# Spectral block on one core: where the second weights' second half is converted, and where the first inverse run stands

## The chip, the cores and the metric

The kernel runs on one core of one Trainium2 chip. The metric is the time of one execution on the device in microseconds (us). Before the change the median of three runs is 1846.89 us (1846.84 to 1847.31). TensorE (PE) multiplies matrices; VectorE (DVE), ScalarE (ACT) and GpSimd (POOL) work on tiles; all DMAs are issued from the queue of SyncE (SP).

## The reference

For x of shape (8, 3136, 256): a real FFT along the sequence, a complex 256x256 channel mix with bias, a soft threshold of 0.01, and the inverse FFT. On its result the second block: u = x + real(FFT2(x)), a layer norm, a two-layer MLP (256 to 1024 to 256) with relu, and the residual. Cut to what matters:

```
X = rfft(x, axis=1)
Y = soft(Xr @ w_r - Xi @ w_i + b_r) + 1j * soft(Xr @ w_i + Xi @ w_r + b_i)
x = irfft(Y, n=3136, axis=1)
u = x + real(fft(fft(x, axis=1), axis=2))
out = u + relu(norm(u) @ w_ch1) @ w_ch2
```

## The kernel before, in words

**Sequences and stages.** The eight sequences (b = 0 to 7) go through ten tasks each, which the code calls p1, p2_f2, p2_w, p2_mix, p2_yt, p2_g2, p3_norm, p3_tr, p3_mlp1 and p3_mlp2. The FFT of 3136 is split into 64 x 49. `p1` is the 64-point step and stores ad (for b = 0: aq) to DRAM. `p2_*` run over q = 0 to 3, four stages of eight frequency slots: `p2_f2` (L503) loads af and the table tff and does the 49-point step (L527), `p2_w` (L559) the channel products g_w, bias and soft threshold (ks L585, y L590, m L592, Y L593), `p2_mix` the channel FFT for the mixed part (ef or eo L631, mq) and its stores md, `p2_yt` (L704) transposes Y (L730), and `p2_g2` the inverse 49-point step, evicted as bev (L761) and stored as bd (L763). `p3_norm` (L774) loads bf from bd and mt from md, does the inverse 64-point step with `quarters` (L405, matmuls L410), adds mt (L779, tile ut) and takes the norm's statistics. `p3_tr` (L847) transposes ut to uth and utl (L861 to L863), `p3_mlp1` (L865) makes h, hh and hl, `p3_mlp2` (L890) makes o and the output. Sequence 0 works in plain fp32; from b = 1 on an operand is a pair of fp32r tiles (h and l) and a product is three matmuls (`mm3`, L170).

**Order.** Each task is a generator that yields due times in units of T. A heap takes the task with the lowest due time, and what it traces up to its next yield comes next; `after(keys)` (L313) puts a task off by 10 of these units until the keys have been marked in `done`. The constants at the top (SHAPE, STEP, T1, WTIMES, NRM, TR and others) set the due times. The framework then fixes the order of each engine, and of SP's queue, in a simulated timeline in which earlier traced work has priority and tiles of one tag get their rooms in turn; on the chip each engine takes its instructions in that order. `tc.issue_after(x)` puts an instruction behind x on the same engine. `behind(key, ...)` (L305) issues a load on SP behind the DMA that `af_ld[key]` names; af_ld[0] to af_ld[7] are the af loads of sequence 0, two for each q.

**The weights.** `weights` (L917) loads the MLP's weights, which come as 64-bit numbers, in eight raw pieces (k = 0 to 7; 0 to 3 for w1, 4 to 7 for w2), and `split_double` (L182) turns a piece into h and l: one activation on ACT (L200), seven operations on DVE (L201, L203, L205, L207, L209, L220, L221) and one cast on ACT (L219). The temporaries are two tiles in the mt rooms (there are two) and two in the ut rooms (there are four). The four pieces of w2 are called its parts 1 to 4 here. Their raw tiles have the two uth rooms; their ACT activation stands behind the last ks of sequence 0's stage q = 2 (parts 1 and 2) or q = 3 (parts 3 and 4). w2's results have the rooms W2 and W3, which `p1` of b = 1 uses for its xf before.

**The first inverse.** For b = 0 the first run of `quarters` is traced after the mark ("w", 1, 0), and its first matmul is put on PE behind the last W product of the second sequence's stage q = 0 (L837, L841). The others are put behind that one.

```
if b == 0 and ms[0] == 0:
    yield from after(("w", 1, 0))
...
quarters(inv_f, groups, w_in[1, 0] if b == 0 and ms[0] == 0 else None)
```

Of the kernel before, what the change touches and what calls it, by code (L numbers as in the profile page):

```python
# [20 lines left out]
D = 256  # L21
# [117 lines left out]
SHAPE, STEP1, STEP = (0.395, 0.569, 0.36), 0.2, 0.25  # L139
START1, LEAD, LAST = 1.61, 1.53, 0.05  # L140
T1, ASK, BEHIND = (1.25, 0.17), 1.16, 3
WTIMES = (1.002, 1.003, 1.151, 1.152, 1.4, 1.44, 1.54, 1.57)
MLAG, NRM, TR = 1.874, -1.239, -0.86


# [1 line left out]
def spectral_block(ctx: ExitStack, tc: tile.TileContext, x, w_ri, b_ri, w1, w2,  # L147
# [169 lines left out]
    def n2_rows(t, m, n):  # L317

        return t[m:m + n].rearrange("n r c u d -> (r c u) n d")
# [183 lines left out]
    def p2_f2(b):  # L503


        for q in range(4):
            base, STEP, F2W, W0, WW, M0 = clock2(b, q)
            u0 = 8 * q
            yield base
            yield from after(("a", b, q) if b == 0 else ("a", b))  # L510
            if b == 0:
                X = sb.tile([128, 2, 2, 8, S], F32, tag=("Xh", "Xl")[q % 2], bufs=1, name="X")
                Xs = sb.tile([128, 2, 8, S], F32, tag=("Xsh", "Xsl")[q % 2], bufs=1, name="Xs")
                xt[b, q] = X, Xs
            else:
                xt[b, q] = Xh, Xl, Xsh, Xsl = x_tiles()
            afs, tfs = zip(*[rows_f2(b, q, s) for s in range(2)])
            for ui in range(4):
                yield base + STEP * ui * F2W / 4
                us = slice(ui * 2, ui * 2 + 2)  # L520
                lo_x = lo_v if b == 1 and q == 0 else lo_g
                g = gtile("g_f2")
                gf = g[:, :400].rearrange("p (k c s j) -> p k c s j", k=2, c=2, s=2)
                for s in range(2):
                    yield base + STEP * F2W * (ui / 4 + s / 8)
                    for k in range(2):
                        mm = te.matmul(gf[:, k, :, s], afs[s][:, ui * D + k * 128:ui * D + k * 128 + 128],  # L527
                                  tfs[s][:, ui].rearrange("p (c j) -> p c j", c=2), start=True, stop=True)
                    if b == 0 and q == 0 and ui == 0:
                        f2_in[s] = mm.ins  # L530
                        done.add(("f2", s))
                gv = g[:, :400].rearrange("p (k c t) -> p k c t", k=2, c=2)

                def view(t):
                    return t[..., us, :].rearrange("p k c s j -> p k c (s j)" if len(t.shape) == 5 else "p k s j -> p k (s j)")

                if b == 0:
                    xv_ = view(X)
                    sc.copy(xv_, gv)
                    va.tensor_add(view(Xs), xv_[:, :, 0], xv_[:, :, 1])  # L540
                    continue
                xs = sb.tile([128, 2, 2 * S], F32, tag="xs", bufs=2, name="xs")
                xh, xl, xsh, xsl = (view(t) for t in (Xh, Xl, Xsh, Xsl))
                if ui < 3:
                    xx = sb.tile([128, 2, 2, 2 * S], F32, tag="xx", bufs=2, name="xx")
                    sc.copy(xx, gv)
                    sc.copy(xh, xx)  # L547
                    lo_x(xl, xx, xh)
                    va.tensor_add(xs, xx[:, :, 0], xx[:, :, 1])
                else:  # L550
                    im = sb.tile([128, 2, 2 * S], F32, tag="im", bufs=1, name="im")
                    sc.copy(xh, gv)
                    sc.copy(im, gv[:, :, 1])
                    va.tensor_add(xs, gv[:, :, 0], im)
                    lo_v(xl, gv, xh)
                sc.copy(xsh, xs)
                lo_x(xsl, xs, xsh)
# [146 lines left out]
    def p2_yt(b):  # L704

        for q in range(4):
            base, STEP, F2W, W0, WW, M0 = clock2(b, q)
            u0 = 8 * q
            yield base + STEP * M0
            y = yt_[b, q]  # L710
            for i in range(4):
                yield base + STEP * (M0 + 0.022 + 0.185 * i)
                s = i // 2
                if i % 2 == 0:
                    tif = sb.tile([100, 4, 98], F32, tag="tif", bufs=2, name="tif")
                    behind(3 if b or q else 1, out=tif, in_=c_ti[:, u0 + 4 * s:u0 + 4 * s + 4, :])
                    if b == 0:
                        tabs[b, q, s] = tif, None
                    else:
                        tih = sb.tile([100, 4, 98], F32R, tag="tih", bufs=1, name="tih")  # L720
                        til = sb.tile([100, 4, 98], F32R, tag="til", bufs=1, name="til")
                        with tc.issue_after(ks_in[b, q]):
                            sc.copy(tih, tif)
                        lo_v(til, tif, tih)
                        tabs[b, q, s] = tih, til
                gt = gtile("g_yt")
                for v in range(2):
                    place = 2 * (2 * (i % 2) + v) + s
                    for o in range(2):
                        te.transpose(gt[:100, (v * 2 + o) * 128:(v * 2 + o + 1) * 128],  # L730
                                     y[:, o, place].rearrange("p c j -> p (c j)"), ident)
                if b == 0:
                    yf = sb.tile([100, 512], F32, tag=("yh", "yl")[i % 2], bufs=2, name="yf")
                    sc.copy(yf, gt[:100])
                    yhl[b, q, i] = yf, None
                    continue
                yh = sb.tile([100, 512], F32R, tag="yh", bufs=2, name="yh")
                yl = sb.tile([100, 512], F32R, tag="yl", bufs=2, name="yl")
                sc.copy(yh, gt[:100])
                lo_v(yl, gt[:100], yh)  # L740
                yhl[b, q, i] = yh, yl
# [32 lines left out]
    def p3_norm(b):  # L774
# [31 lines left out]
        def load(m, n):  # L806
            mt = sb.tile([128, 4, D], F32, tag="mt", bufs=2, name="mt")
            bfs = [sb.tile([128, 512], F32, tag="bf", bufs=4, name="bf") for _ in range(1 + (n > 1))]
            for r in range(2):
                if n == 1:  # L810
                    nc.sync.dma_start(out=bfs[0][64 * r:64 * r + 64, :D], in_=b_dram[b - 1 + r][m, 0].rearrange("c u d -> (c u) d"))
                else:
                    nc.sync.dma_start(out=bfs[r].rearrange("p (n d) -> p n d", d=D), in_=n2_rows(b_dram[b], m + 2 * r, 2))
            for r in (1, 0):
                bb, n2 = (b - 1 + r, m) if n == 1 else (b, NM * r + m)
                mpn, mmn = (d[0:NH].rearrange("(a n2) d -> a n2 d", n2=N2) for d in m_dram[bb])
# [6 lines left out]
        for ms in pairs + [[NM - 1]] * (b % 2):  # L823
            n = 1 if ms[0] == NM - 1 else 4
            t0, T3 = clock3(b, ms[0])
            yield t0 + T3 * (NRM - 0.5 * (n == 1))
            yield from after(("b", b), ("m", b))
            loads = [load(m, n) for m in ms]
            if n == 1:
                mt, bfs = loads[0]  # L830
                g = gtile("g_g1")
                te.matmul(g[:, :D], inv_f, bfs[0][:, :D], start=True, stop=True)
                add(ms[0], 1, g, mt[:, :1])
                finish(ms[0], 1)
                continue
            if b == 0 and ms[0] == 0:
                yield from after(("w", 1, 0))  # L837
            groups = [([gtile("g_g1") for _ in range(2)], [[bfs[r][64 * p:64 * p + 64] for r in range(2)] for p in range(2)], bfs[0][0:1, 0:2])
                      for mt, bfs in loads]
            quarters(inv_f, groups, w_in[1, 0] if b == 0 and ms[0] == 0 else None)  # L840
            parts = [(m + 2 * p, g, mt[:, 2 * p:2 * p + 2]) for m, (mt, bfs), (banks, movs, late) in zip(ms, loads, groups) for p, g in enumerate(banks)]  # L841
            for m, g, mt in parts:
                add(m, 2, g, mt)
            for m, g, mt in parts:
                finish(m, 2)

    def p3_tr(b):  # L847
        for gi, (g0, z) in enumerate(GROUPS[b % 2]):
            t0, T3 = clock3(b, g0)
            w = z * 128  # L850
            for k in range(2):
                yield t0 + T3 * (TR + k / 4)
                if k == 0:
                    uth = sb.tile([128, 2, 512], F32R, tag="uth", bufs=UTHB, name="uth")
                    utl = sb.tile([128, 2, 512], F32R, tag="utl", bufs=2, name="utl")
# [61 lines left out]
    def weights():  # L917
# [8 lines left out]

        def load(k):
            i, name, sl, src = todo[k]
            tag = "utl" if k in (2, 3) else "uth"
            raw = raws[k] = sb.tile([128, 1024], I32, tag=tag, bufs=2 if tag == "utl" else UTHB, name="raw_" + name)  # L930
            behind(("q1", "q1", 3, 3, 5, 5, 5, 5)[k], out=raw.rearrange("p (f e) -> p f e", f=src.shape[1]), in_=src)
        for k, (i, name, sl, src) in enumerate(todo):
            yield T * WTIMES[k]
            yield from after("q1")
# [4 lines left out]
                l = sb.tile(shape, F32R, tag=f"W{2 * i + 1}", bufs=1, name=name + "l")  # L939
                mlp_w[name] = h, l  # L940
            if i:
                split_double(name, h, l, [(sl, raws.pop(k))], False, ks_in[0, 2 + (k > 5)])
            elif k % 2:
                mark = (0, k // 2)
                yield from after(("w",) + mark)
# [69 lines left out]
```

## Time and profile before

| | |
|---|---|
| median of three runs | 1846.89 us |
| the profiled execution's own time | 1843.13 us |
| its span, first to last instruction | 1841.2 us |
| mean granted TensorE clock | 0.993 |
| PE busy | 1798.6 us, 98% |
| DVE busy | 1200.5 us, 65% |
| ACT busy | 807.7 us, 44% |
| POOL busy | 561.8 us, 31% |

Times in the rows are microseconds from the span's start. In a timeline, each line has the start, the duration, the engine, the line of the kernel, the operation, the tiles and a count; what stands in brackets is the idle time of the engine before it and what ended that. Neighbouring instructions of an engine overlap a little. The profiled execution is one run; its own time stands 3.76 us below the median of the others.

### The profile page before, as it was taken

The page shows a single profiled execution, that of the slowest core. Times are in us where ns is not written, and L with a number is a line of the kernel's source. Part 1 is how long each engine was busy: PE and PEld are TensorE (multiplying, and loading weights), DVE is VectorE, ACT ScalarE, POOL GpSimd, SP SyncE. Part 2 cuts the span into 40 slices and gives each one's busy share as a digit, 9 for nine tenths or more (in the row PEclk, how much of TensorE's full clock was granted, in tenths as well). Part 3 has the DMA queues.
Part 4 walks back from the last instruction along what each step waited for, and adds up shares of the span by engine and source line. Part 5 has one row for each costly group of instructions (what it writes and reads, how often), then busy time and mean ns, then how long its engine had stood idle before and what let it go on. Part 6 is the DMA issues. An engine that isn't in the chain of part 4 may idle for free.

```text
span 1841.2 us, 29453 instructions
## 1 busy us (share of the span) xinstructions
PE 1798.6 (98%) x10087; PEld 1498.7 (81%) x10087; DVE 1200.5 (65%) x2619; ACT 807.7 (44%) x1911; POOL 561.8 (31%) x1021
## 2 busy tenths in 40 slices
PE   8987999999999999999999999999999999999998
PEld 5566778888888988888888888888888898878888
DVE  3685686676577766765776667757657767655543
ACT  2664545444445534444444444444444454432222
POOL 0002434333234333343432343423324344222110
PEclk9998999999999999999999999999999999999999
DMA  8856564444436543374515744346533533152211
GB/s 247 272 173 165 165 178 135 148 137 138 130 82 198 159 123 104 97 212 125 172 47 135 215 132 125 104 129 164 159 99 86 169 94 112 56 150 69 59 35 33
DMA packets 157934, 245.61 MB, mean 133 GB/s; under 512 B 24208, under 2 KB 105176, under 8 KB 157528
## 3 DMA queue, kind: packets, MB, share of 16 engines
q1 hardware_dynamic: 157784, 243.72, 45.3%
q8 instruction: 80, 1.31, 0.3%
q14 instruction: 70, 0.57, 0.1%
HBM read 140.79 MB, written 102.86 MB: 132 GB/s over the span
## 4 chain that ended last, share of the span: by engine, by line
PE 86%; DVE 5%; DMA 4%; ACT 1%; SPq 1%; issue 1%; POOL 1%; DVEq 0%; ACTq 0%; POOLq 0%
PE o L175 28%; PE h L175 27%; PE g_w L175 9%; PE g_f L527 5%; PE g_g L175 4%; PE g_yt L730 3%; PE g_g L410 2%; PE g_ut L861 2%; PE g_f L410 2%; PE g_mix L667 1%; DMA out_dram<-total 1%; PE g_f L372 1%; DMA aq<-ev 1%; PE g_mix L669 1%; PE g_w L576 1%
## 5 line engine op out<-in xcount | busy, mean ns | idle before, releaser
L880 DVE SCALAR_TENSOR_TENSOR hl<-h,hh 128x512 fp32r<-128x512 f32 (+2 forms) x416 | 272.1, 655 | 391.2 <-ACT hh L879 386.8
L879 ACT ACTIVATE hh<-h 128x512 fp32r<-128x512 f32 (+2 forms) x416 | 237.7, 572 | 505.7 <-PE h L175 459.4
L175 PE MATMUL o<-hl,w2h 128*128 128x512 f32 (+2 forms) x832 | 328.9, 395 | 2.0 <-DVE hl L880 1.5
L175 PE MATMUL h<-utl,w1h 128*128 128x512 f32 (+2 forms) x832 | 319.0, 383 | 1.3 <-DVE utl L165 1.3
L175 PE MATMUL o<-hh,w2l 128*128 128x512 f32 (+2 forms) x832 | 317.9, 382 | 0.0
L175 PE MATMUL o<-hh,w2h 128*128 128x512 f32 (+2 forms) x832 | 317.3, 381 | 0.0
L175 PE MATMUL h<-uth,w1l 128*128 128x512 f32 (+2 forms) x832 | 316.0, 380 | 0.0
L175 PE MATMUL h<-uth,w1h 128*128 128x512 f32 (+2 forms) x832 | 315.3, 379 | 0.0
L887 POOL TENSOR_TENSOR total<-uth,utl 128x256 f32<-128x256 f32 x200 | 149.6, 772 | 460.6 <-DMA out_dram<-total 244.9
L175 PEld LDWEIGHTS o<-hl,w2h 128*128 128x128 f32 x832 | 156.7, 188 | 49.3 <-DVE hl L880 18.7
L175 PEld LDWEIGHTS h<-utl,w1h 128*128 128x128 f32 x832 | 156.8, 188 | 30.5 <-DVE utl L165 1.7
L175 PEld LDWEIGHTS h<-uth,w1l 128*128 128x128 f32 x832 | 156.7, 188 | 29.5 <-issue 1.6
L175 PEld LDWEIGHTS h<-uth,w1h 128*128 128x128 f32 x832 | 156.9, 189 | 27.7 <-issue 2.4
L175 PEld LDWEIGHTS o<-hh,w2l 128*128 128x128 f32 x832 | 156.5, 188 | 27.2
L175 PEld LDWEIGHTS o<-hh,w2h 128*128 128x128 f32 x832 | 156.9, 189 | 19.8 <-issue 0.8
L527 PE MATMUL g_f<-tff,af 98*128 98x100 f32 x1024 | 139.9, 276 | 2.1 <-DMA af<-aq 1.3
L527 PEld LDWEIGHTS g_f<-tff,af 98*128 98x128 f32 x1024 | 134.2, 195 | 7.8 <-issue 1.7
L593 POOL TENSOR_TENSOR Y<-y,m 128x400 f32<-128x400 f32 x56 | 66.9, 1194 | 208.4 <-DVE m L592 198.6
L590 DVE SCALAR_TENSOR_TENSOR y<-g_w,small,ks 128x400 f32<-128x400 f32 x128 | 80.4, 629 | 54.3 <-PE g_w L175 38.0
L168 POOL TENSOR_TENSOR Xl<-xx,Xh 128x400 fp32r<-128x400 f32 x81 | 88.4, 1092 | 60.3 <-ACT Xh L547 56.8
L761 ACT COPY bev<-g_g 98x512 f32<-98x512 f32 x128 | 74.7, 585 | 40.2 <-PE g_g L175 29.3
L730 PE MATMUL g_yt<-ident,Y 128*100 128x128 f32 x512 | 81.8, 277 | 4.8 <-DVE Y L593 4.6
(162 smaller groups left out, 3269.7 us busy)
## 6 DMA issues: line engine op xcount, KB each, us to landing
bd<-bev SPq DMA_DIRECT2D x128, 196.0 KB
mt<-md SPq DMA_DIRECT2D x192, 128.0 KB
bf<-bd SPq DMA_DIRECT2D x96, 256.0 KB
out_dram<-total SPq DMA_DIRECT2D x88, 256.0 KB
af<-ad SPq DMA_DIRECT2D x56, 392.0 KB
ad<-xf SPq DMA_DIRECT2D x84, 256.0 KB
md<-mq SPq DMA_DIRECT2D x112, 192.0 KB
xf<-in_x SPq DMA_DIRECT2D x39, 512.0 KB
```

The source lines that it names most:

```text
L168: gp.tensor_sub(out_, full, hi.bitcast(F32))
L175: last = te.matmul(o, l, r, start=start and i == 0, stop=stop and i == 2)
L410: return te.matmul(banks[i][64 * j:64 * j + 64], mat[rows, rows], movs[i][j], start=True, stop=True)
L527: mm = te.matmul(gf[:, k, :, s], afs[s][:, ui * D + k * 128:ui * D + k * 128 + 128], tfs[s][:, ui].rearrange("p (c j) -> p c j", c=2), sta ...
L590: va.scalar_tensor_tensor(y1, gw, bias[:, c, o:o + 1], ks, op0=ALU.add, op1=ALU.add)
L593: (va if b == 0 or o == 0 else gp).tensor_sub(y[:, o, :, c, :], y1, m)
L730: te.transpose(gt[:100, (v * 2 + o) * 128:(v * 2 + o + 1) * 128], y[:, o, place].rearrange("p c j -> p (c j)"), ident)
L761: sc.copy(bev, g[:98])
L861: te.transpose(gv[:, i], ut[:, j, k * 128:(k + 1) * 128], ident)
L879: sc.activation(hh[:, :w], h[:, :w], AF.Relu)
L880: va.scalar_tensor_tensor(hl[:, :w], h[:, :w], 0.0, hh[:, :w].bitcast(F32), op0=ALU.max, op1=ALU.subtract)
L887: gp.tensor_add(total[:, k, cols], uth[:, k, cols].bitcast(F32), utl[:, k, cols].bitcast(F32))
```

## The change

Parts 1 and 2 of w2 are placed behind ks of stage q = 1 and q = 2 of sequence 0 (before: q = 2 for both); parts 3 and 4 behind the last ks of stage q = 0 of the second sequence (before: q = 3 of sequence 0). The raw tiles of parts 3 and 4 get the two tot rooms, and their loads follow af_ld[7] in place of af_ld[5]. The task waits for the W stage's mark before it traces a conversion. The first inverse run is traced, and put on PE, behind the last f2 matmul of the second sequence's stage q = 1. The tif loads of the second sequence's stage q = 0 are traced after the first load of `p3_norm` and issued behind its bf load; the first transposes of u are traced after the first group of `p3_norm`. Four due times of w2's parts change.

```diff
-WTIMES = (1.002, 1.003, 1.151, 1.152, 1.4, 1.44, 1.54, 1.57)
+WTIMES = (1.002, 1.003, 1.151, 1.152, 1.36, 1.42, 1.6, 1.61)
...
@@ p2_f2
                         f2_in[s] = mm.ins
                         done.add(("f2", s))
+                    if b == 1 and q == 1 and ui == 3 and s == 1:
+                        f2_in["last"] = mm.ins
+                        done.add("f2")
...
@@ p2_yt
                 if i % 2 == 0:
+                    if b == 1 and q == 0:
+                        yield from after("norm")
                     tif = sb.tile([100, 4, 98], F32, tag="tif", bufs=2, name="tif")
-                    behind(3 if b or q else 1, out=tif, in_=c_ti[:, u0 + 4 * s:u0 + 4 * s + 4, :])
+                    behind("bf" if b == 1 and q == 0 else 3 if b or q else 1, out=tif, in_=c_ti[:, u0 + 4 * s:u0 + 4 * s + 4, :])
...
@@ p3_norm
-                    nc.sync.dma_start(out=bfs[r].rearrange("p (n d) -> p n d", d=D), in_=n2_rows(b_dram[b], m + 2 * r, 2))
+                    af_ld["bf"] = nc.sync.dma_start(out=bfs[r].rearrange("p (n d) -> p n d", d=D), in_=n2_rows(b_dram[b], m + 2 * r, 2)).ins
...
             loads = [load(m, n) for m in ms]
+            done.add("norm")
...
             if b == 0 and ms[0] == 0:
-                yield from after(("w", 1, 0))
+                yield from after("f2")
...
-            quarters(inv_f, groups, w_in[1, 0] if b == 0 and ms[0] == 0 else None)
+            quarters(inv_f, groups, f2_in["last"] if b == 0 and ms[0] == 0 else None)
...
             for m, g, mt in parts:
                 finish(m, 2)
+            done.add(("n", b))
...
@@ p3_tr
                 yield t0 + T3 * (TR + k / 4)
+                if b == gi == 0:
+                    yield from after(("n", 0))
...
@@ weights
-            tag = "utl" if k in (2, 3) else "uth"
-            raw = raws[k] = sb.tile([128, 1024], I32, tag=tag, bufs=2 if tag == "utl" else UTHB, name="raw_" + name)
-            behind(("q1", "q1", 3, 3, 5, 5, 5, 5)[k], out=raw.rearrange("p (f e) -> p f e", f=src.shape[1]), in_=src)
+            tag = ("uth", "utl", "uth", "tot")[k // 2]
+            raw = raws[k] = sb.tile([128, 1024], I32, tag=tag, bufs=2, name="raw_" + name)
+            behind(("q1", "q1", 3, 3, 5, 5, 7, 7)[k], out=raw.rearrange("p (f e) -> p f e", f=src.shape[1]), in_=src)
...
             if i:
-                split_double(name, h, l, [(sl, raws.pop(k))], False, ks_in[0, 2 + (k > 5)])
+                mark = ((0, 1), (0, 2), (1, 0), (1, 0))[k - 4]
+                yield from after(("w",) + mark)
+                split_double(name, h, l, [(sl, raws.pop(k))], False, ks_in[mark])
```

## Rows read from the trace of the kernel before

**Rows 1.** Busy time in stretches: length, busy per engine, PE clock, DMA share, GB/s.
```profile
60.00:80.00 20.00, 19.28 (x115) 11.81 (x113) 15.85 (x36) 12.16 (x31) 0.00 (x0) 1.00 0.78 255
...
96.00:107.00 11.00, 8.21 (x59) 6.78 (x58) 10.44 (x26) 7.32 (x17) 0.00 (x0) 1.00 0.85 256
114.00:129.00 15.00, 9.56 (x45) 7.04 (x44) 13.93 (x36) 7.95 (x20) 0.00 (x0) 0.80 0.30 84
145.40:153.10 7.70, 0.31 (x3) 0.04 (x1) 2.49 (x6) 0.15 (x1) 1.33 (x2) 0.83 0.98 263
153.10:164.20 11.10, 9.84 (x44) 7.79 (x44) 7.66 (x21) 6.18 (x13) 5.32 (x9) 0.50 0.79 184
300.00:400.00 100.00, 100.00 (x554) 83.67 (x553) 67.55 (x148) 45.55 (x109) 34.61 (x65) 1.00 0.47 141
```

**Rows 2.** Timeline of PE at the end of the first sequence.
```profile
114.48 0.61 PE L664 MATMUL g_mix<-csf,ef 128*100 128x129 f32 x4
...
116.27 1.51 PE L576 MATMUL g_w<-X,wdf 128*128 128x400 f32 x4
...
121.70 0.87 PE L664 MATMUL g_mix<-csf,ef 128*100 128x129 f32 x6 [2.51 <-DVE mq L676]
124.64 0.88 PE L730 MATMUL g_yt<-ident,Y 128*100 128x128 f32 x3 [2.06 <-DVE Y L593]
126.38 2.54 PE L664 MATMUL g_mix<-csf,ef 128*100 128x129 f32 x10 [0.86 <-ACT yf L734]
```

**Rows 3.** Timeline of DVE: first and last of part 4's seven operations.
```profile
119.86 0.42 DVE L201 TENSOR_SCALAR cv_w_mt<-cv_w_mt 128x512 f32<-128x512 f32 x1
...
127.56 0.69 DVE L221 TENSOR_TENSOR w2l<-cv_w_ut 128x512 fp32r<-128x512 f32 x1
```

**Rows 4.** The chain that ended last, 130 to 176 us: start, us, what.
```profile
134.93 4.91 DMA md<-mq
...
142.10 0.56 SPq L763
142.70 3.40 DMA bd<-bev
...
146.60 6.36 DMA bf<-bd
```

**Rows 5.** Timeline of PE around the first inverse.
```profile
129.57 2.12 PE L527 MATMUL g_f<-tff,af 98*128 98x100 f32 x16
...
153.09 2.10 PE L410 MATMUL g_g<-bf,inv_f 64*64 64x512 f32 x8 [7.39 <-DMA bf<-bd]
...
155.36 3.58 PE L527 MATMUL g_f<-tff,af 98*128 98x100 f32 x16
...
164.22 0.80 PE L175 MATMUL h<-utl,w1h 128*128 128x512 f32 x1 [1.28 <-DVE utl L165]
```

**Rows 6.** Timeline of ACT: the last bev of sequence 0, the second sequence's ks.
```profile
137.43 1.15 ACT L761 COPY bev<-g_g 98x512 f32<-98x512 f32 x2
...
143.55 0.49 ACT L585 COPY ks<-g_w 128x400 f32<-128x400 f32 x1 [0.42 <-PE g_w L175]
```

**Rows 7.** Timeline of DVE between the second sequence's first W stage and the add.
```profile
143.17 1.18 DVE L590 SCALAR_TENSOR_TENSOR y<-g_w,small,ks 128x400 f32<-128x400 f32 x2 [3.94 <-ACT ks L585]
...
147.33 0.63 DVE L590 SCALAR_TENSOR_TENSOR y<-g_w,small,ks 128x400 f32<-128x400 f32 x1
155.22 1.29 DVE L779 TENSOR_TENSOR ut<-g_g,mt 128x512 f32<-128x512 f32 x2 [7.26 <-PE g_g L410]
```

**Rows 8.** Timeline of SP's queue: the ad stores out of W3, the first mt load.
```profile
82.06 1.42 SPq L470 DMA_DIRECT2D ad<-xf  x2
...
139.97 0.69 SPq L818 DMA_DIRECT2D mt<-md  x1
```

**Rows 9.** The span and the mean granted clock.
```profile
core 0: 1841.2 us, clock 0.993
```

**Rows 10.** Instructions of line 168 on POOL, 140 to 180 us: ns min/median/max.
```profile
L168 POOL TENSOR_TENSOR Xsl<-xs,Xsh x4: 607/714/967, 161.5 to 171.5; 128x200 fp32r<-128x200 f32 x4
L168 POOL TENSOR_TENSOR Xl<-xx,Xh x3: 1035/1057/1238, 158.4 to 165.8; 128x400 fp32r<-128x400 f32 x3
```

## The prediction

> **What bounds the kernel now.** First the table of stretches. From 300 to 400 us TensorE (PE) is busy 100.00 of 100 us at the full clock [rows 1], so from there on PE bounds the kernel, and an edit in the ramp is worth the PE time that it saves before, idle or at half clock, and no more. The reader is to see two holes in the ramp. From 114 to 129 us PE is busy 9.56 of 15 us and VectorE (DVE) 13.93: DVE bounds the end of the first sequence. From 145.4 to 153.1 us PE does nearly nothing, and in the 11.1 us behind it PE has the lower clock level, 0.50, that is 1.2 of 2.4 GHz [rows 1].
>
> PE's instructions say what it waited for in the first hole: 2.51 us for DVE's mq, 2.06 for DVE's Y, 0.86 for ScalarE (ACT), 5.4 together; the ten mix matmuls behind take 2.54 us, where four took 0.61 before, so 1.0 us is lost at half clock [rows 2]. The hole is worth 6.4 us at most. Among DVE's instructions there are two conversions of second weights. One of them runs from 119.86 to 128.2 us: three operations of 0.42 us and four of 0.69 [rows 3], 4.0 us as recorded, 3.5 net, since neighbours overlap by some 0.08.
>
> The chain of waits names the second hole: md stores land after 4.91 us, bd stores go out at 142.10 and land after 3.40, the bf loads after 6.36 [rows 4]. PE, which has its program in a fixed order, waits 7.39 us for them in front of the first inverse; the f2 matmuls of the second stage behind it take 3.58 us for 16, against 2.12 in the first stage [rows 5]. In the half-clock stretch PE is busy 9.84 us [rows 1]; half is lost, 4.9. The hole is worth 7.4 + 4.9 = 12.3 us at most.
>
> **The change, part by part.** (a) Parts 1 and 2 of the second weights go one W stage forward. Where part 2 is now (96 to 107 us) DVE is busy 10.44 of 11 us and PE idle 2.8 [rows 1]: a gain of 0 to 2.8. Part 1 goes into 60 to 80 us, where DVE is busy 15.85 of 20 and PE 19.28 [rows 1]; 3.5 us more nearly fill DVE: a cost of 0 to 3.5, and no gain there, as work is only added. Both are equally near, so I take 0 for (a).
>
> (b) Parts 3 and 4 leave the tail. Behind the last W product, which ends at 117.8 us [rows 2], nine of their fourteen operations are left, 4.7 us of DVE's time until 128.2. What stays in the chain is DVE's own Y, ef and mq, and ACT's copies. At most the 5.4 us of waits go, and the loss at half clock with them; at least nothing. I take 4.5 of 6.4: most of the waits are on DVE, but one is on ACT, and each mix step keeps its links through PE and ACT.
>
> (c) The same two parts come back behind the second sequence's first W stage, behind ACT's ks at 143.55 [rows 6]. DVE has its y, m and Y there until 148 and then stands idle 7.26 us in front of the inverse's add [rows 7]; the conversions, 2 x 3.5 = 7.0, just fit. But they take the two mt rooms and the four ut rooms, which the inverse needs for its mt tile and its sums. The first mt room is free for a load once part 4 has read it: with DVE never idle from 143.2 us (4.8 of its own and 7.0 of conversions, less the last four operations, 2.1) that is 152.9 at the latest; if the conversions go first, 148. Four mt issues of 0.69 [rows 8] and a landing as for bd (3.40 [rows 4]) bring the add to between 154 and 159, against 155.22 now [rows 7].
>
> (d) The first inverse moves behind the f2 matmuls of the second stage: 32 of them, 4.2 us by twice the first stage's row [rows 5]. They fill over half of PE's wait. And on the SP queue the mt loads stand ahead of the bd stores now and hold them while they wait for md to land: mt at 139.97 [rows 8], bd at 142.10 [rows 4], though ACT was done with the bev for them at 138.6 [rows 6]. If the mt loads become possible only behind the conversions, bd can go out 3.5 us earlier, and the second stage's af, queued behind, with it. 7.4 - 4.2 - 3.5 leaves no wait at the inverse itself, and without the hole the clock should stay up. What is late next is the add (c), and with it the transposes and the first MLP matmul, now at 164.22 [rows 5], 9.0 us behind the add. Some 5 of those 9.0 are f2 at half clock (24 of them by their row [rows 5]), which would be done by then, so the MLP should start between 158 and 163. Until then PE has the inverse, the Y transposes and the second stage's W products, whose inputs come earlier too. I keep 5.8 us of loss for waits on DVE and take 6.5 of 12.3; the ends are 0 and 12.3.
>
> What moves at no cost: the raw loads of parts 3 and 4 now follow the eighth af load and have some 30 us until the conversion. The two tif loads go behind the bf loads; their product is wanted first by the second sequence's g2, behind the first MLP matmuls. The mark ahead of the transposes only orders the tracing. The first o matmuls that need parts 3 and 4 come some 25 us behind the conversion. Without that cover each would cost one landing, 3 to 6 us [rows 4].
>
> **Sum.** 0 + 4.5 + 6.5 = 11 us off the profiled execution's own 1843.1 (its span is 1841.2 [rows 9], with 1.9 around it) gives 1832.1. The median of the runs is 1846.9, 3.8 above that execution, so the forecast in runs is 1836.
>
> **The rivals.** A: DVE becomes the wait. From 143 to 160 us it has 7.0 us more, and f2's second stage brings GpSimd (POOL) into the same stretch: three Xl of 1.06 us and four Xsl of 0.71, the slowest 0.97 where the quickest is 0.61 [rows 10]. In the first sequence the conversions had no POOL work beside them (0.00 in each of its stretches [rows 1]). If the two take turns, up to 6 us are added to DVE's 11.8, the MLP starts no earlier than now and only (b) is left: 1843.1 - 4.5 + 3.8 = 1842.4. The spread of the POOL rows speaks for it; against it, that POOL's work begins only when f2's results have been evicted. The Trainium skill ("SBUF — State Buffer", Who interferes with whom) states that VectorE and GpSimd share one port pair under an exclusive lock, taken among others by a VectorE operation with two SBUF inputs against a GpSimd operation that reads SBUF, and that the loser blocks fully. By that rule alone this rival would be the likely one; the trace agrees only so far as one Xsl is 0.36 us longer than another, and shows no Xl blocked for a whole operation.
>
> B: Part 1, earlier now, waits in DVE's order for the room W3, which the second sequence's first stage empties with stores at 82.06 us [rows 8]; by bd's 3.40 they land near 86.4 (issue 0.9), and an estimate, four fifths into the stretch of (a), has DVE at part 1's last operation by 76. Ten us of waiting in DVE's queue, with the first sequence's Y and mq behind it, eat the gain: 1843.1 - 1 + 3.8 = 1846. For it: DVE takes its instructions in order. Against it: that order comes from a simulated timeline in which those stores are known.
>
> C: Slower. The mt loads keep their place on SP ahead of the bd stores. Then they wait for part 4, until 152.9 instead of 139.97, and the 13.1 us from there to the inverse follow: it runs at 166. PE idles from 145.7 on, less 4.2 for f2: 16.1 us against 7.4, 8.7 more, with the half clock behind it as now. With (b): 1843.1 + 8.7 - 4.5 + 3.8 = 1851.1. It decides once the mt loads hold bd for longer than the 4.2 us that f2 covers. Against it: the order of a queue follows the rooms, and rooms that come free late put the loads back.
>
> **How the numbers follow.** A measurement of this kernel tells 0.2% (3.7 us) from no change. The forecast (a gain of 4 to 19) has 0.55, A 0.18, B 0.12, C 0.15. Faster is the forecast's 0.55 and 0.11 of A, whose 4.5 us lie just beyond the bound: 0.66. Same is 0.07 of A and 0.10 of B: 0.17. Slower is C and the rest of B: 0.17. The range begins at 1828, where (b) and (d) give all that they can (6.4 + 12.3), and ends at 1850, which leaves out most of C and the little beyond 19. The forecast's own range is 1828 to 1843.
>
> **What would show it.** Right: in the changed profile PE's waits for mq and Y at the first sequence's end are under 2 us together, with the full clock there; the second stage's f2 stands ahead of the first inverse, and no stretch at 0.50 follows; bd stores go out ahead of the mt loads; the first MLP matmul comes some 10 us earlier. Wrong: a wait of PE on DVE's ut or utl of over 5 us (A); a DVE wait at 76 to 86 us that the ad stores end (B); bd stores held on SP behind mt (C). The prediction falls if PE is still at half clock behind the inverse, or if PE is no longer full after 300 us.

## The result, and the profile after

The changed kernel takes 1859.16 us (median of four executions, 1856.79 to 1863.36), the kernel before, measured beside it, 1846.87 us: a ratio of 1.0073, 95% interval 1.0050 to 1.0095. It is slower, by 12.3 us, and lies outside the range. The profiled execution's span, 1854.9 us at a mean clock of 0.988, is 13.7 us longer than that of [rows 9]; its own time is 1856.79 us.

The table of stretches of the changed kernel (length, busy per engine, PE clock, DMA share, GB/s), for [rows 1]:

```profile
60.00:80.00 20.00, 15.18 (x66) 8.81 (x64) 16.42 (x39) 8.36 (x20) 0.00 (x0) 0.91 0.63 203
114.00:129.00 15.00, 14.13 (x66) 9.48 (x64) 8.28 (x21) 5.62 (x14) 0.00 (x0) 1.00 0.53 178
145.00:158.88 13.88, 5.54 (x31) 5.20 (x30) 5.71 (x13) 3.17 (x6) 0.10 (x1) 0.86 0.60 184
159.00:180.00 21.00, 13.31 (x62) 11.13 (x62) 17.30 (x29) 10.52 (x24) 8.86 (x10) 0.50 0.35 102
300.00:400.00 100.00, 100.00 (x564) 82.42 (x563) 70.05 (x154) 46.75 (x112) 35.86 (x73) 1.00 0.51 158
```

From 300 to 400 us PE is full, as before, so the loss lies in the ramp. PE has 15.18 us in 60 to 80, where it had 19.28. From 114 to 129 it is at the full clock and busy for 14.13 us, but the stretch now holds work that comes later than before. From 145 us to 158.88 it works 5.54 us, and from 159 to 180 its clock is 0.50.

PE's timeline of the changed kernel, for [rows 2, 5] (new lines: 667 is mix, 735 the transposes of Y, 870 those of u):

```profile
124.08 1.51 PE L579 MATMUL g_w<-X,wdf 128*128 128x400 f32 x4
...
127.29 0.87 PE L667 MATMUL g_mix<-csf,ef 128*100 128x129 f32 x6 [0.29 <-DVE ef L634]
128.75 0.54 PE L735 MATMUL g_yt<-ident,Y 128*100 128x128 f32 x3 [0.58 <-DVE Y L596]
129.96 0.46 PE L667 MATMUL g_mix<-csf,ef 128*100 128x129 f32 x2 [0.67 <-ACT yf L739]
131.62 2.03 PE L667 MATMUL g_mix<-csf,ef 128*100 128x128 f32 x8 [1.20 <-ACT ef L637]
...
143.71 0.45 PE L175 MATMUL g_w<-Xsh,wrh 128*128 128x400 f32 x1 [0.30 <-ACT Xsh L559]
...
158.88 0.45 PE L735 MATMUL g_yt<-ident,Y 128*100 128x128 f32 x1 [8.35 <-POOL Y L603]
...
173.25 0.53 PE L175 MATMUL g_g<-yl,tih 100*98 100x256 f32 x1 [5.14 <-DVE yl L165]
...
178.84 1.99 PE L410 MATMUL g_g<-bf,inv_f 64*64 64x512 f32 x8 [0.78 <-ACT low L676]
...
187.48 0.40 PE L175 MATMUL h<-utl,w1h 128*128 128x512 f32 x1
```

The reader is to see three distances. The last W product of the first sequence starts at 124.08, not at 116.27: **7.8 us lost** before the stretch that the change was about. From there to the second sequence's first W product it is 19.6 us (124.08 to 143.71), where it was 22.6 (that product started at 138.88): **3.0 gained**; the four waits there add up to 2.7 us instead of 5.4, and mq is gone from them. Behind it come a wait of 8.35 us for Y and one of 5.14 for yl, the first inverse runs at 178.84 instead of 153.09, and the MLP starts at 187.48 instead of 164.22.

What ended the 8.35 us stands in the chain that ended last (start, duration, what):

```profile
144.28 7.34 DMA bd<-bev
...
152.89 4.07 DMA tif<-c_ti
...
156.98 0.53 ACT tih L728
...
157.53 0.57 DVE til L165
158.10 0.48 DVE Y L596
```

The tif load landed at 157.0. ACT's tih waits for it, DVE's til for tih, and DVE's Y stands behind til; PE's transposes wait for Y. On SP's queue, for [rows 8]:

```profile
143.83 1.02 SPq L768 DMA_DIRECT2D bd<-bev  x2
...
152.89 0.80 SPq L309 DMA_DIRECT2D tif<-c_ti  x2
...
166.28 0.69 SPq L823 DMA_DIRECT2D mt<-md  x1
```

The bd stores do go out before the mt loads, which come at 166.28, and bf and tif follow the landing of bd. But bd took 7.34 us to land, not 3.40 [rows 4].

Of the 7.8 us, 1.7 are half clock at 52 to 56 us, which the profile of the kernel before doesn't have and which stands ahead of the wait that follows. Most of the rest begins on ACT: part 1's activation holds ACT until its raw load is there.

```profile
68.14 0.66 ACT L200 ACTIVATE cv_w_mt<-raw_w 128x512 f32<-128x512 f32 x1 [3.32 <-DMA raw_w<-in_w]
```

**An account of the ramp.** For each kernel below: the start of the second sequence's first W product (column W), and what PE lost in the 80 us behind it: idle time, and busy time x (1 - granted clock), both summed over 40 stretches of 2 us. W plus the loss explains the span: the span less both is 1684.9 to 1688.6 us for all of them but one (1691.2, parts 1 and 2 alone).

| kernel | last W of seq. 0 | W | idle | half clock | W + loss | span |
|---|---|---|---|---|---|---|
| before | 116.27 | 138.88 | 9.5 | 6.6 | 154.9 | 1841.2 |
| changed | 124.08 | 143.71 | 17.0 | 9.1 | 169.9 | 1854.9 |
| 1: tif as before | 124.93 | 144.56 | 13.3 | 5.9 | 163.7 | 1851.7 |
| 2: parts 1, 2 back | 116.52 | 135.72 | 16.5 | 10.1 | 162.3 | 1850.0 |
| 3: both back | 117.07 | 136.37 | 11.6 | 9.0 | 157.0 | 1845.6 |
| 4: inverse alone | 120.39 | 143.00 | 9.8 | 9.1 | 161.9 | 1847.8 |
| 5: parts 3, 4 alone | 118.08 | 139.61 | 10.5 | 5.2 | 155.2 | 1840.4 |
| 6: as 3, two f2 steps | 117.67 | 139.09 | 8.1 | 6.8 | 154.0 | 1840.8 |
| 7: as 3, three steps | 119.27 | 139.77 | 11.5 | 5.5 | 156.8 | 1841.7 |
| 8: as 4, two steps | 119.23 | 142.16 | 6.1 | 6.5 | 154.8 | 1842.7 |
| 9: as 6, less POOL | 120.18 | 141.72 | 7.5 | 6.0 | 155.2 | 1841.4 |
| 10: parts 1, 2 alone | 125.93 | 148.64 | 12.9 | 4.5 | 165.9 | 1857.1 |
| 11: as 10, raw early | 121.05 | 144.24 | 9.1 | 4.5 | 157.8 | 1844.0 |
| 12: as 9, no POOL | 118.80 | 138.27 | 6.7 | 6.3 | 151.2 | 1836.5 |

Each row is one profiled execution, with its own luck in the clock of the first 114 us (last section). Each ratio below compares all executions of a kernel with those of the kernel before that were measured beside them.

### The profile page after: what moved, and what is told of

It is laid out like the page before. It is cut to its first block, busy times and chain, and to the rows that moved or that the text cites. A ratio compares the mean times of both kernels' runs of the same rounds, so it can differ in the third digit from the quotient of the medians.

```text
span 1854.9 us, 29447 instructions
## 1 busy us (share of the span) xinstructions
PE 1805.2 (97%) x10087; PEld 1502.7 (81%) x10087; DVE 1203.6 (65%) x2619; ACT 808.1 (44%) x1911; POOL 562.6 (30%) x1021
## 4 chain that ended last, share of the span: by engine, by line
PE 87%; DVE 5%; DMA 4%; ACT 2%; SPq 1%; issue 1%; POOL 1%; DVEq 0%; ACTq 0%
PE o L175 28%; PE h L175 27%; PE g_w L175 9%; PE g_f L527 5%; PE g_g L175 4%; PE g_yt L735 3%; PE g_g L410 2%; PE g_ut L870 2%; PE g_f L410 2%; PE g_mix L670 1%; PE g_w L579 1%; DMA raw_w<-in_w 1%; DMA aq<-ev 1%; PE g_mix L672 1%; DMA out_dram<-total 1%
## 5 line engine op out<-in xcount | busy, mean ns | idle before, releaser
L735 PE MATMUL g_yt<-ident,Y 128*100 128x128 f32 x512 | 83.5, 281 | 12.9 <-POOL Y L603 9.6
```

## The experiments

Runs 1 to 4 undo parts of the change, or do one alone.

**Run 1, the tif loads as before.** Against the changed kernel:

```diff
-                    if b == 1 and q == 0:
-                        yield from after("norm")
...
-                    behind("bf" if b == 1 and q == 0 else 3 if b or q else 1, out=tif, ...)
+                    behind(3 if b or q else 1, out=tif, ...)
```

> The changed kernel, but the two tif loads of the second sequence's stage q = 0 go out as before the change, not behind the bf loads. Theory 1 (a late table blocks DVE): PE's wait of 8.35 us at the second stage's first Y transpose comes from til, which stands in DVE's order ahead of Y and waits for tif; without it that wait is under 1 us and the time falls from 1859 by 6 to 9 us, to 1850 to 1853. Theory 2 (DVE's load and POOL beside it): the conversions' own work and the collisions with POOL fill the same time; the wait moves to yl or ut and the time falls by under 2 us. Theory 3 (the inverse's late place) expects under 2 us too.

Measured: 1854.34 us, 1.0058 (1.0043 to 1.0073). PE's timeline:

```profile
154.29 0.32 PE L733 MATMUL g_yt<-ident,Y 128*100 128x128 f32 x1 [2.91 <-POOL Y L603]
...
168.68 0.53 PE L175 MATMUL g_g<-yl,tih 100*98 100x256 f32 x1 [5.14 <-DVE yl L165]
```

The wait for Y falls from 8.35 to 2.91 us, the 5.14 for yl stays. By the ratios that is worth 0.15% (2.8 us), with intervals that overlap; run 2 below, against run 3, gives 0.27% (5.0), with intervals that do not. The tif loads are a cost, less than theory 1's 6 to 9 us, and less than half of the loss.

**Run 2, parts 1 and 2 as before; run 3, these and tif as before.** Run 2 against the changed kernel, run 3 with run 1's edit as well:

```diff
-WTIMES = (1.002, 1.003, 1.151, 1.152, 1.36, 1.42, 1.6, 1.61)
+WTIMES = (1.002, 1.003, 1.151, 1.152, 1.4, 1.44, 1.6, 1.61)
...
-                mark = ((0, 1), (0, 2), (1, 0), (1, 0))[k - 4]
-                yield from after(("w",) + mark)
+                mark = ((0, 2), (0, 2), (1, 0), (1, 0))[k - 4]
+                if k - 4 in (2, 3):
+                    yield from after(("w",) + mark)
```

> The changed kernel, but parts 1 and 2 of the second weights are converted where they were before (behind stage q = 2). Theory 1: part 1's activation waits on ACT for its raw load (3.32 us) and holds DVE and PE behind it; with it back the last W product of the first sequence ends near 118 us as before, not 127, and the time falls by 6 to 9 us from 1859, to 1850 to 1853. Rival (the ramp's first 100 us differ by chance from run to run, half clock at 52 to 56 us among it): the W product stays at 124 or later and the time falls by under 2 us.

> Both undone: what stays is parts 3 and 4 in the second sequence and the first inverse behind the second stage. Theory 1: both losses go, the time is 1841 to 1846, at or below the kernel before (1847). Theory 2: what is left of the second stage's loss, some 7 us, stays: 1850 or more. Theory 3: the same as theory 2, but the wait stands in front of the inverse and the first MLP matmul.

Measured: run 2 1851.56 us, 1.0035 (1.0020 to 1.0049); run 3 1846.52 us, 1.0008 (0.9998 to 1.0017). With parts 1 and 2 back, the last W product starts at 116.52 and 117.07 again. That is 0.38% (changed kernel against run 2) to 0.50% (run 1 against run 3). What is left in run 3, moving parts 3 and 4 and the inverse, still gains nothing, where theory 1 had it at or below the kernel before. PE's timeline of run 3:

```profile
166.08 1.99 PE L410 MATMUL g_g<-bf,inv_f 64*64 64x512 f32 x8 [0.78 <-DVE Xl L165]
```

**Run 4, the inverse alone behind all four f2 steps; run 5, parts 3 and 4 alone.** In run 4 the weights and tif are as before; in run 5 only the weights' parts 3 and 4 move, and the inverse is where it was. Run 5's edit of the inverse, against the changed kernel:

```diff
-                yield from after("f2")
+                yield from after(("w", 1, 0))
...
-            quarters(inv_f, groups, f2_in["last"] if b == 0 and ms[0] == 0 else None)
+            quarters(inv_f, groups, w_in[1, 0] if b == 0 and ms[0] == 0 else None)
```

> The kernel before with only the first inverse moved behind the second stage's f2 (and the marks for it); all conversions and tif loads as before. Theories 1 and 2: f2 fills PE's wait of 7.4 us, no half clock behind it: 4 to 10 us faster than before, 1837 to 1843. Theory 3: the inverse lands behind the Y transposes and g2 in PE's order, so the add, the transposes and the MLP start late: same as before or up to 6 us slower, 1847 to 1853.

> The kernel before with parts 3 and 4 converted in the second sequence (tot rooms, behind the second sequence's first W stage); inverse, tif and parts 1 and 2 as before. If the late place of the inverse is what eats the gain, this keeps the 3 to 4 us of the first sequence's end and the inverse comes as soon as bf lands, near 150 us: 1838 to 1843 against 1845.4 before. If DVE's load in the second sequence eats it (conversions and POOL side by side), it is 1845 to 1850 and DVE has no gap from the ks on until 160 us.

Measured: run 4 1848.55 us, 1.0018 (1.0008 to 1.0027), slower by itself; run 5 1843.84 us, 0.9999 (0.9987 to 1.0011). PE's timeline of run 4:

```profile
157.39 2.88 PE L527 MATMUL g_f<-tff,af 98*128 98x100 f32 x12 [3.14 <-DMA tff<-c_tf]
...
170.62 1.99 PE L410 MATMUL g_g<-bf,inv_f 64*64 64x512 f32 x8 [0.78 <-ACT low L676]
```

The inverse runs at 170.62, 17.5 us later than in [rows 5]. Between the third and the fourth f2 step PE's order has six transposes of Y and six g2 matmuls, which wait for yl, and in and behind the fourth step it has four mix matmuls and four more transposes. "Behind the last f2" means behind all of these, on both kernels (run 3: 166.08). In run 4 the f2 matmuls also wait for their table, 3.14 us. Run 5 does not keep the 3 to 4 us that its expectation gave the first sequence's end (W to W gains 1.1), and its time doesn't differ from that of the kernel before.

**Runs 6, 7 and 8, the inverse behind two or three of the four steps.** Run 6 is run 3 with the inverse behind the second step, run 7 behind the third, run 8 is run 4 behind the second:

```diff
-                    if b == 1 and q == 1 and ui == 3 and s == 1:
+                    if b == 1 and q == 1 and ui == 1 and s == 1:
```

> As the run with parts 3 and 4 and the inverse moved (1846.5), but the inverse stands behind the second of the four f2 steps of the second stage instead of the fourth. Place in PE's order decides: the inverse runs near 152 us instead of 166, the add 6 to 10 us earlier, the time falls by 3 to 6 us, to 1840 to 1843, under the kernel before. DVE's load decides: the inverse runs early, but the add stays behind the conversions, near 160 us or later, and the time falls by under 2 us.

> As the last one, behind the third f2 step. Place decides: the inverse near 154 us, the time within 1 us of the run behind the second step. DVE's load decides: within 2 us of 1846.5.

> The kernel before, only the first inverse moved, behind the second f2 step; conversions as before. Against the run behind the fourth step (1848.6): place decides: 1841 to 1845, as f2 fills part of PE's 7.4 us and the inverse follows at once when bf has landed. If f2's inputs (af, tff) land no earlier than bf, nothing is filled: 1845 to 1848.

Measured: run 6 1841.96 us, 0.9988 (0.9977 to 1.0000); run 7 1843.81, 0.9997 (0.9987 to 1.0006); run 8 1843.07, 0.9996 (0.9985 to 1.0008). By the ratios, the step by which the inverse is placed is worth 0.20% (run 3 against run 6) and 0.22% (run 4 against run 8). Run 7, with the inverse at 158.82 us, not near 154, fits neither of its two expectations. PE's timeline of run 6:

```profile
154.27 1.99 PE L410 MATMUL g_g<-bf,inv_f 64*64 64x512 f32 x8 [1.42 <-ACT xx L549]
...
161.69 2.03 PE L527 MATMUL g_f<-tff,af 98*128 98x100 f32 x8 [3.64 <-DVE ut L782]
```

The inverse waits for no transfer, and the loss behind W is 14.9 us (8.1 + 6.8) against 16.1 before; in run 8 it is 12.6. What PE now waits for is DVE's add (ut), 3.64 us. Two things in front of the add end together there: DVE's own operations, and its mt tile. The mt loads go out when part 4's L205 is done, at 156.2, on SP's queue:

```profile
156.21 0.69 SPq L821 DMA_DIRECT2D mt<-md  x1
```

The fourth of them, issued at 158.20, landed at 160.82 (the chain that ended last), and the add starts at 160.94.

**Run 9, DVE in place of POOL.** DVE is busy without a gap in run 6 from 145 us to 164. DVE's timeline of run 6, and POOL's beside it:

```profile
150.79 1.20 DVE L221 TENSOR_TENSOR w2l<-cv_w_ut 128x512 fp32r<-128x512 f32 x1
151.91 0.41 DVE L203 TENSOR_SCALAR cv_w_mt<-cv_w_mt 128x512 int32<-128x512 int32 x1
152.25 1.19 DVE L552 TENSOR_TENSOR xs<-xx 128x200 f32<-128x200 f32 x1
...
155.09 1.09 DVE L205 SCALAR_TENSOR_TENSOR cv_w_ut<-raw_w,cv_w_mt 128x512 int32<-128x512 int32 x1
```

```profile
150.41 1.03 POOL L596 TENSOR_TENSOR Y<-y,m 128x400 f32<-128x400 f32 x1 [1.65 <-DVE m L595]
152.09 1.12 POOL L168 TENSOR_TENSOR Xl<-xx,Xh 128x400 fp32r<-128x400 f32 x1 [0.65 <-ACT g_g L411]
...
154.90 0.73 POOL L168 TENSOR_TENSOR Xsl<-xs,Xsh 128x200 fp32r<-128x200 f32 x1
155.59 1.48 POOL L168 TENSOR_TENSOR Xl<-xx,Xh 128x400 fp32r<-128x400 f32 x1
```

DVE's xs, 0.36 us elsewhere, takes 1.19: POOL's Xl runs from 152.09 to 153.21, and xs ends 0.23 behind it. L221 and L205 (0.68 alone) end 0.55 behind Y and Xsl. L203, which has one input tile, starts 0.18 us ahead of Xl and takes 0.41 as ever. That does not mean that one input tile spares it: in run 7 it starts while an Xl runs, and ends 0.28 behind that one (DVE, then POOL; run 1 has 1.25 in the same place):

```profile
152.60 1.24 DVE L203 TENSOR_SCALAR cv_w_mt<-cv_w_mt 128x512 int32<-128x512 int32 x1
```

```profile
152.09 1.47 POOL L168 TENSOR_TENSOR Xl<-xx,Xh 128x400 fp32r<-128x400 f32 x1
```

The other way about, POOL's second Xl in run 6 takes 1.48 us, as it starts while L205 runs until 156.18. Run 9 gives the subtractions of the second stage to DVE; against run 6:

```diff
-                lo_x = lo_v if b == 1 and q == 0 else lo_g
+                lo_x = lo_v if b == 1 and q <= 1 else lo_g
...
-                    (va if b == 0 or o == 0 else gp).tensor_sub(y[:, o, :, c, :], y1, m)
+                    (va if b == 0 or o == 0 or b == q == 1 else gp).tensor_sub(y[:, o, :, c, :], y1, m)
```

> Parts 3 and 4 in the second sequence and the first inverse behind two f2 steps, as in the kernel before this one in the series, but the second stage's Y and X subtractions are VectorE's instead of GpSimd's. Theory 1 (VectorE's operations stretch because GpSimd works beside them): xs falls from 1.19 back to 0.37 us, L205 and L209 from 1.09 to 0.69, L221 from 1.20 to 0.69; that gives back 3.7 us and costs 2.5 for the six subtractions that VectorE now has, so the inverse's add comes about 1.2 us earlier than 160.9 and the time is 1 to 2.5 us under the 0.9988 of that kernel: 0.9975 to 0.9985. Theory 2 (they stretch for another reason, such as the loads under way): the long operations stay, VectorE has 2.5 us more, 1.0000 to 1.0010.

Measured: 1839.88 us, 0.9977 (0.9965 to 0.9989). DVE's timeline of run 9, and the two subtractions that POOL still had:

```profile
153.44 1.19 DVE L221 TENSOR_TENSOR w2l<-cv_w_ut 128x512 fp32r<-128x512 f32 x1
...
154.89 0.35 DVE L552 TENSOR_TENSOR xs<-xx 128x200 f32<-128x200 f32 x1
...
155.44 1.53 DVE L634 SCALAR_TENSOR_TENSOR eo<-Y,mask 128x200 f32<-128x200 f32 x2
156.90 0.68 DVE L205 SCALAR_TENSOR_TENSOR cv_w_ut<-raw_w,cv_w_mt 128x512 int32<-128x512 int32 x1
```

```profile
153.05 1.03 POOL L596 TENSOR_TENSOR Y<-y,m 128x400 f32<-128x400 f32 x1 [1.65 <-DVE m L595]
155.60 1.15 POOL L596 TENSOR_TENSOR Y<-y,m 128x400 f32<-128x400 f32 x1 [1.52 <-DVE m L595]
```

xs is at 0.35 and L205 at 0.68 again, as theory 1 has it. L221 and eo are still long, and they lie where POOL's Y runs. The add comes 20.8 us behind W (162.49 less 141.72) against 21.9 (160.94 less 139.09) in run 6, though DVE has four subtractions more ahead of it (two Xl, two Xsl); the order differs as well, with one el more ahead of the add and the last L221 (0.67 us) behind it. This kernel is faster than the kernel before (0.23%), and so than the changed one.

**Run 12, these two as well.** Against run 9:

```diff
-                    (va if b == 0 or o == 0 or b == q == 1 else gp).tensor_sub(y[:, o, :, c, :], y1, m)
+                    (va if b == 0 or o == 0 or b == 1 and q < 2 else gp).tensor_sub(y[:, o, :, c, :], y1, m)
```

> As the run without GpSimd's subtractions in the second stage, and the last two Y subtractions of the first W stage are VectorE's as well, so that between 140 and 165 us GpSimd has no subtraction left. Theory 1 (VectorE's operations stretch exactly where GpSimd works): the two that were still long there, L221 at 1.19 us and the two eo at 1.53, fall to 0.69 and 0.76; that gives back 1.3 us and costs 1.0, so the time stays within 1 us of that run: 0.9970 to 0.9985. Theory 2 (these operations are long where they stand, whatever GpSimd does): L221 and eo stay at 1.19 and 1.53 and the time is 1 us up: 0.9980 to 0.9990.

Measured: 1841.37 us, 0.9979 (0.9965 to 0.9992), the same as run 9. DVE's timeline:

```profile
149.98 0.68 DVE L221 TENSOR_TENSOR w2l<-cv_w_ut 128x512 fp32r<-128x512 f32 x1
...
151.40 0.36 DVE L552 TENSOR_TENSOR xs<-xx 128x200 f32<-128x200 f32 x1
...
153.04 0.76 DVE L634 SCALAR_TENSOR_TENSOR eo<-Y,mask 128x200 f32<-128x200 f32 x2
```

L221 is at 0.68 and the two eo at 0.76: the long operations went with POOL's subtractions, one by one. The mt loads go out at 152.39 here, and the add, at 158.22, waits for DVE's own operations alone.

**Runs 10 and 11, parts 1 and 2.** Run 10 is the kernel before with these two alone moved; run 11 is run 10 with part 1's raw load earlier:

```diff
-            behind(("q1", "q1", 3, 3, 5, 5, 5, 5)[k], ...)
+            behind(("q1", "q1", 3, 3, 3, 5, 5, 5)[k], ...)
```

> Only parts 1 and 2 go one W stage forward; all else as before. Theory 1 (part 1's activation waits for its raw load on ScalarE and holds what is queued behind it): PE busy in 60 to 80 us falls from 19.28 to 15 to 16, the last W product of the first sequence starts some 7 us later than 116.3, the time is 6 to 9 us up: 1.0035 to 1.0050. Theory 2 (parts 1 and 2 cost only together with the other edits): under 1.0020.

> As the run with parts 1 and 2 alone, but part 1's raw load stands behind the fourth af load instead of the sixth, so that it can be there some 8 us sooner. Theory 1 (the late raw load is the cause): ScalarE's wait of 3.3 us on raw_w is gone, PE is busy over 18 us in 60 to 80, the time is at most 1.0020. Theory 2 (VectorE has no room there): PE stays at 15 to 16.5 in 60 to 80 and the time at 1.0035 to 1.0050.

Measured: run 10 1856.10 us, 1.0066 (1.0046 to 1.0087); run 11 1848.70 us, 1.0027 (1.0013 to 1.0041). ACT's timeline in run 10, then in run 11:

```profile
69.31 0.66 ACT L200 ACTIVATE cv_w_mt<-raw_w 128x512 f32<-128x512 f32 x1 [5.58 <-DMA raw_w<-in_w]
```

```profile
62.47 0.68 ACT L200 ACTIVATE cv_w_mt<-raw_w 128x512 f32<-128x512 f32 x1 [0.56 <-DVE cv_w_ut L205]
```

With the load earlier, ACT's wait for it (5.58 us in run 10) is gone, PE is busy for 17.51 us in 60 to 80 instead of 14.51, and 0.39% of the 0.66% are back. So the load is the larger cause, but run 11 lies between the two theories: PE is 1.8 us short of its 19.28 in that stretch, waits 1.14 us for DVE's Y there, and DVE has no gap from 56.6 to 76.1 us, as theory 2 has it. More of what is left shows on DVE and PE of run 11:

```profile
89.51 0.69 DVE L221 TENSOR_TENSOR w2l<-cv_w_ut 128x512 fp32r<-128x512 f32 x1 [2.99 <-DMA ad<-xf]
```

```profile
90.81 1.94 PE L579 MATMUL g_w<-X,wdf 128*128 128x400 f32 x4 [2.54 <-DVE mq L679]
```

DVE's last operation of part 1 waits for the ad stores that empty W3, the first sequence's mq stands behind it, and PE waits 2.54 us for that: the prediction's rival B.

## Why the prediction was wrong

**(a) Parts 1 and 2: wrong, and the largest loss.** The step took 0, with a bound of 3.5, from how full DVE is. It costs 0.38 to 0.66%, 7 to 12 us. It had moved the activation on ACT and its seven DVE operations but not asked when their input is there: the raw load still goes out behind the sixth af load, and everything behind the activation on ACT, and behind L201 on DVE, waits with it (run 10, run 11). Rival B is part of the 0.27% that run 11 keeps, and how large a part no run shows. It was placed at 76 to 86 us; DVE's wait for the ad stores ends at 89.5 in run 11 and at 94.2 in the changed kernel.

**(b) The first sequence's tail: right in kind, the size smaller.** 4.5 us were forecast; the waits fell by 2.7, and W to W by 3.0 (changed kernel). The gain spreads from 1.1 to 3.4 (runs 5, 6 and 7: 21.5, 21.4 and 20.5; runs 2 and 3: 19.2 and 19.3): between the two W products PE's idle time falls from 6.5 to between 2.8 and 3.5 us in all of them, but the half clock there takes between 1.4 and 4.8 us, where it took 2.3. The term was to recover the clock loss as well.

**(c) Parts 3 and 4 in the second sequence: "just fit" failed.** The 7.26 us gap in front of the add was DVE's only room, and its operations do not keep their lengths beside POOL. In run 6 the stretched ones add 3.8 us (xs 2 x 0.83, L221 0.5, L205 and L209 0.4 each, eo 0.8). This is rival A: its mechanism is shown by runs 9 and 12. The Trainium skill ("SBUF — State Buffer", Who interferes with whom) had said so: a VectorE instruction with two SBUF inputs contends with a GpSimd instruction that reads SBUF, one with at most one such input does not unless it is in a two-port mode, which a tensor_scalar can enter, and the one that is issued second is blocked. The trace agrees: 0.36 became 1.19 us for xs, and L203, a tensor_scalar, took 0.41 us where it was first and 1.24 where Xl was (run 7); that L203 is in such a mode no run shows. The prediction looked at POOL's rows alone and found it weak; DVE's own timeline of the kernel before had it, el at 0.56 us where it starts ahead of POOL's subtraction and at 1.09 where it starts behind that of an Xl (DVE, then POOL):

```profile
161.28 0.56 DVE L165 TENSOR_TENSOR el<-eo,eh 128x400 fp32r<-128x400 f32 x1
...
166.24 1.09 DVE L165 TENSOR_TENSOR el<-eo,eh 128x400 fp32r<-128x400 f32 x1 [0.51 <-ACT eh L637]
```

```profile
165.84 1.06 POOL L168 TENSOR_TENSOR Xl<-xx,Xh 128x400 fp32r<-128x400 f32 x1
```

Rival A is not all of it. In run 12, where nothing is stretched, the add still comes 20.0 us behind W, and it was 16.3 before; the six subtractions that DVE took over ahead of it are 2.5 of these 3.6 us (an estimate: four of 0.57 and two of 0.36, less 0.08 of overlap each). The mt room was to be free by 152.9 us, 14.0 behind W: the mt loads go out 22.6 us behind W in the changed kernel, 17.1 in run 6, and only in run 12 at 14.1. The 5.14 us wait for yl in the changed kernel stands behind DVE's conversions and the stretched operations too: the chain that ended last runs over DVE from 157.53 to 170.92 us.

**(d) The inverse behind f2: wrong in where the last f2 stands.** "They fill over half of PE's wait" took the 32 f2 matmuls as ready and next to each other. The fourth step stands behind transposes and g2, so the inverse came 13 us later than before even in run 3, and alone it costs 0.18% (run 4). Behind two steps the same idea works: behind W, run 8 loses 12.6 us where the kernel before loses 16.1, 3.5 of the 6.5 forecast; by the ratios, runs 6 and 8 can't be told from no change. That bd leaves ahead of mt was right: the last one's transfer begins at 144.28, 0.6 us behind the start of W, where it was 142.70 [rows 4], 3.8 us behind. It gained nothing, since the landing grew from 3.40 to 7.34 us. That no wait stands at the inverse was right too (0.78), and that the clock stays up was not (0.50 from 159 to 180).

**"What moves at no cost".** The tif loads cost 2.8 to 5.0 us. That their product is wanted late is true; but the conversion til stands in DVE's order ahead of Y, and a late load stops all that DVE has behind it. The raw loads of parts 3 and 4 cost nothing that the traces show; the mark ahead of the transposes wasn't tried by itself.

**The rivals.** C had the sign, and not the mechanism: the mt loads did not hold bd. A was there and is worth 0.11% by the ratios (run 9 against run 6, whose intervals overlap). B had 10 us of loss from part 1, near what (a) cost, but from the room W3, not from the raw load. No rival had (a), the tif loads and (d) together, and the sum had 0 for the first two and a gain for the third.

## What to carry to other kernels

When work is moved to an earlier place on in-order engines, ask first when its input lands, on which engine the first instruction waits, and what is queued behind it there; the idle time of the engine that does most of the work is no bound on that cost. "Behind X" costs all that the order has ahead of X: read the neighbours in the timeline before pinning something to the last of a series. Before filling an engine's gap, look for the same operations in the trace with and without the other engine beside them.

## What the runs showed of the hardware

**POOL and DVE take turns by the instruction.** In runs 6 and 7 a blocked DVE operation ends 0.23 to 0.55 us behind POOL's, 0.13 less than its own length of 0.36, 0.41 or 0.68. One that reads PSUM keeps its length: in run 6 utl starts at 165.55, beside an Xl that runs from 165.10 to 166.14, and takes 0.68 us as elsewhere. Giving six subtractions to the busier engine made its add come sooner (20.0 us behind W in run 12, 21.9 in run 6), in part because the last L221 stands behind the add there.

**The clock of the same instructions differs from execution to execution.** Runs 4 and 8 have the same instructions on PE until the second sequence's second stage. PE waited 2.22 us in front of its first f2 matmuls in run 4, 0.52 in run 8. The first 40 us of run 4, then of run 8:

```profile
0.00:40.00 40.00, 32.33 (x102) 21.05 (x103) 7.63 (x16) 9.13 (x16) 0.21 (x4) 0.87 0.78 228
```

```profile
0.00:40.00 40.00, 33.36 (x117) 20.15 (x117) 9.50 (x21) 9.40 (x17) 0.20 (x4) 1.00 0.84 252
```

The granted clock is 0.87 against 1.00. The wait alone doesn't decide: behind one of 1.17 us in the same place (run 6) the clock fell to 0.50, behind one of 1.33 (run 11) it stayed at 1.00. The half clock takes 6.3 and 4.7 us in the first 114 us of these executions, and nothing in that of the kernel before. So a single profile of such a ramp can be some 6 us off, as much as the largest term of the sum, and only the ratios over many executions told the edits apart.
